# A banded attention, a gated MLP and a mixer on one core: weight conversions at other places, a reciprocal one group earlier

## The chip, the cores and the metric

The kernel runs on one core of one Trainium2 chip. The metric is the device time of one execution in microseconds, as a median of several. The core has five engines that run on their own and meet through semaphores: TensorE (PE, matrix products), VectorE (DVE), ScalarE (ACT), GpSimd (POOL) and SyncE (SP), which here only issues DMA transfers. Each engine takes its instructions strictly in the order in which the program has them, so an instruction that waits holds all that stand behind it.

## The reference

Three parts run one after another on 2 batches of 768 tokens. First an attention with 8 heads of 64, in which a query sees the last `window` keys and the first `n_sink`; then a gated MLP with a spatial gate; then a token and channel mixer.

```python
scores = np.where(keep, scale * q @ k.T, -1e9)            # keep: sinks, or 0 <= rel < window
a = np.exp(scores - max); a = a / (a.sum(-1) + 1e-09)
x = (a @ v) over the heads side by side                   # (2, 768, 512)
h = np.maximum(x @ w_in, 0.0);  u, v = h[..., :512], h[..., 512:]
v_n = (v - mean) / np.sqrt(var + 1e-06)
v_s = np.einsum('ts,bsd->btd', w_spatial, v_n) + b_spatial[None, :, None]
x = (u * v_s) @ w_out
u = x + (np.maximum(x.T @ w_tok1, 0.0) @ w_tok2).T        # token mixing
out = u + np.maximum(u @ w_ch1, 0.0) @ w_ch2              # channel mixing
```

The weights come as 64-bit floats; each 128 x 512 piece is turned into a 32-bit float and then split into a high and a low part, and each product is made of three matmuls (high by high, high by low, low by high).

## The kernel before

**The attention loop** (`banded`) runs over n from -3 to 25. Group n is half of the 8 heads of one block of 128 queries: j = n // 2 is the block (12 of them, 6 for each batch), ph = n % 2 the half. It is a hand-written software pipeline. One pass of the loop issues, in this order: the loads for later blocks (odd n); the reciprocal of the sums of group n+1 (`sums`, L198, VectorE); the transposes of group n (L272, TensorE) and their copies out (L280 on ScalarE, L283 on VectorE); the scaling of two heads of group n+1 on GpSimd (`norm`, L250); the second half of the last weight conversion (`flush`, L506 on ScalarE and L507 on GpSimd); the scaling of the two other heads on ScalarE (L255); the score products of group n+3 (L191) and their masking and minimum on VectorE (L215, L220); the exponentials of group n+2 on ScalarE with their sums (L236, L240); the products with v of group n-1 (L306); and, in even passes, the output of block j-1: `x_out` with L334 on ScalarE and L335 on VectorE. The accumulator `pv` of the products with v has one PSUM buffer, so that the products of the next block wait for L335.

**A weight conversion** (`pump`) takes three operations on VectorE (L488, L492, L495); its `flush` comes one conversion or one pass later: a rounding copy on ScalarE (L506) and a subtraction on GpSimd (L507). Before its work `pump` issues the next load (`prefetch`) on SP's queue, two loads ahead at most. In the loop `pump` is called at the end of the passes in `PUMPS`, eight times: four pieces of `w_in` for v, then four for u.

**The fills.** While attention runs, TensorE also gets the products of the gated MLP, in steps: a v tile (`v_tile`, 128 tokens, four steps of three matmuls of 512 columns, then relu L539, statistics L549 and normalisation L554) and a u tile (`u_tile`, 384 tokens, four steps of 384 columns). A list `self.fills` fixes their order; each pass takes steps from its head up to `BUDGET`, and only if the block that the head needs is done (`xdone`). What is left over runs after the loop.

**After the loop** come the spatial gate, the product with `w_out` (`x2_tile`), the token mixing (`tok1_tile`, `tok2_tile`, with the addition L633 on VectorE) and the channel mixing, three chunks of twelve tiles f: `ch1_tile` (L653 on ScalarE, L654 on VectorE make the two parts of the activated tile) and `ch2_part` of the tile before. The other 38 conversions are called in these stages, each at a fixed place.

Of the kernel before, what the change touches and what calls it, by code (L numbers as in the profile page):

```python
# [29 lines left out]
NG = B * NB * 2  # L30

LQ, LE, LN = 3, 2, 1
PUMPS = range(-1, 7)
BUDGET = 1900


def f32(ap):
    return ap.bitcast(F32)


class Kernel:
# [302 lines left out]
    def banded(self):  # L344
        self.q, self.vb, self.vsb, self.ps_s, self.ss, self.e, self.sm, self.rs = {}, {}, {}, {}, {}, {}, {}, {}
        self.aT, self.ps_x, self.aS, self.dv, self.eS = {}, {}, {}, {}, {}
        NJ = B * NB
        self.kr = self.ap.tile([P, NC4, RING, KW], F32, name="kr")
        self.vf = self.ap, "vf", 2
        self.scalar_loads(self.cp)  # L350
        self.load_qk(0, 2)
        self.warm(10)
        self.load_qk(1)
        self.prefetch()
        self.load_v(0)
        self.load_qk(2)
        self.masks(self.ap)
        for n in range(-LQ, NG + 2):
            j, ph = divmod(n, 2)
            self.xdone = self.xnext  # L360
            if ph and n >= -1:
                if (n + 7) // 2 < NJ:
                    self.load_qk((n + 7) // 2)
                if (n + 3) // 2 < NJ:
                    self.load_v((n + 3) // 2)
            if 0 <= n + LN < NG:
                self.sums(n + LN)
            if 0 <= n < NG:
                self.a_transpose(n)
                self.a_out(n)  # L370
            if 0 <= n + LN < NG:
                self.norm(n + LN, "P")
            if n - 1 in PUMPS:
                self.flush()
            if 0 <= n + LN < NG:
                self.norm(n + LN, "A")
            if n + LQ < NG:
                self.qk(n + LQ)
                if n < 0:
                    self.warm(3)  # L380
                self.scores(n + LQ)
            if 0 <= n + LE < NG:
                self.expo(n + LE)
            if 0 <= n - 1 < NG:
                self.pv(n - 1)
                if ph == 0:
                    if (j - 1) % NB:
                        self.sinks_mm(j - 1)

                    self.fill_until(j - 1)  # L390
                    self.x_out(j - 1)
            if 0 <= n < NG and ph == 0 and j % NB:
                self.v_step(j)
                self.sink_parts(j)
            if n in (2, 3, 14, 15):
                self.split_vs(n // 12, n % 2)
            self.step()
            if n in PUMPS:
                self.pump()
            if 0 <= n < NG and ph == 1 and j % NB:  # L400
                self.sinks(j)
            if n == NG - 4:
                self.raws = [self.spatial_load(r) for r in range(2)]
            self.fill(BUDGET)
        self.xdone = self.xnext
        self.vf = self.sp, "tmp", 4


    def start_x(self):

        self.xT = self.pair(("XH", "XL"), [P, NC4, S], "xT")
        self.w_v = self.pair(("WA", "WB"), [P, NC4, 512], "wv")
        self.w_u = self.pair(("UC", "UD"), [P, NC4, 512], "wu")
        self.wq, self.wstarted, self.wdone, self.half = [], 0, 0, None
        for c in range(NC4):
            self.queue_weight(self.w_in, slice(c * P, c * P + P), (512, 1024), tuple(x[:, c] for x in self.w_v))
        for c in range(NC4):
            self.queue_weight(self.w_in, slice(c * P, c * P + P), (0, 512), tuple(x[:, c] for x in self.w_u))
        self.vn = [self.pair((f"{x}H", f"{x}L"), [P, NB, 512], "vn") for x in "VN"]
        self.uT = [self.unit(f"U{b}", [P, NC4, S], F32, "uT") for b in range(B)]  # L420
        self.xdone = self.xnext = -1
        self.raws = []
        self.later = []

        self.fills = []
        for b in range(B):
            for half in range(2):
                for t in range(3 * half, 3 * half + 3):
                    self.fills.append((b * NB + t, b * NB + t, self.v_tile(b, t)))
                for d in range(NC4):  # L430
                    self.fills.append((b * NB + 3 * half + 2, b * NB + 3 * half, self.u_tile(b, d, half)))
# [41 lines left out]
    def pump(self, n=1):  # L473
        for _ in range(n):
            self.prefetch()
            if self.wdone >= len(self.wq):
                self.flush()
                return
            src, rows, (c0, c1), (dh, dl), raw = self.wq[self.wdone]
            n_ = c1 - c0  # L480
            V = self.nc.vector
            if src.dtype == F32:
                w = raw[:, :n_]
            else:
                r3 = raw.rearrange("p (c w) -> p c w", w=2)
                lo, hi = r3[:, :n_, 0], r3[:, :n_, 1]
                wi = self.sp.tile([P, 512], I32, name="wi", tag="tmp", bufs=4)[:, :n_]
                V.tensor_scalar(  # L488
                    out=wi, in0=hi, scalar1=3, scalar2=0x3FFFFFFF,
                    op0=ALU.logical_shift_left, op1=ALU.bitwise_and,  # L490
                )
                V.scalar_tensor_tensor(  # L492
                    out=wi, in0=hi, scalar=-0x40000000, in1=wi, op0=ALU.bitwise_and, op1=ALU.bitwise_or
                )
                V.scalar_tensor_tensor(  # L495
                    out=wi, in0=lo, scalar=29, in1=wi, op0=ALU.logical_shift_right, op1=ALU.bitwise_or
                )
                w = f32(wi)
            self.flush()
            self.half = w, dh, dl  # L500
            self.wdone += 1
# [168 lines left out]
    def mlp(self):  # L670
        pump = self.pump
# [77 lines left out]
        for n, (b, t) in enumerate(BT):  # L749
            self.tok2_tile(b, t)  # L750
            if 6 <= n <= 9:
                self.u_transpose(n - 6)
            if n == 0:
                self.flush()
            if n >= 9:
                pump()

        self.u2T += [self.pair(("XH", "XL"), [P, NC4, 512], "u2")]
# [2 lines left out]
        for n in range(NCH * NF + 1):  # L761
            if n < NCH * NF:
                ch, f = divmod(n, NF)
                if ch == 1 and f == 0:
                    self.u2T += [self.pair(("NH", "NL"), [P, NC4, 512], "u2")]
                self.ch1_tile(ch, f)
                if ch == 0:
                    pump()
                if 3 <= f < 7 and ch + 1 < NCH:
                    self.u_transpose(4 * (ch + 1) + f - 3)  # L770
            if n >= 1:
                self.ch2_part(*divmod(n - 1, NF))
# [163 lines left out]
```

## Time and profile before

| what | value |
|---|---|
| median of 3 runs | 488.09 us (488.01 to 489.81) |
| the profiled execution | 488.14 us, of which the span from first to last instruction is 486.4 us |
| TensorE busy | 465.6 us, 96% of the span |
| VectorE, ScalarE, GpSimd busy | 273.9, 183.2, 143.5 us |
| load of a piece of `w_in`, issue to landing (median) | 4.5 us |
| load of a piece of `w_ch1` or `w_ch2`, issue to landing (median) | 3.5 us |

How to read it: the span stands 1.7 us below the execution's own time, which is what lies around the first and the last instruction. Busy shares are means over stages with different limits: the attention loop takes the first 135 us, and there the shares are quite different from those of channel mixing, which begins at about 278 us. Matmuls are pipelined, so their listed lengths overlap; the starts of neighbours tell how fast they follow each other.

### The profile page before, as it was taken

What the parts mean: (1) busy time and instruction counts of PE and PEld (TensorE: products, weight loads), DVE (VectorE), ACT (ScalarE), POOL (GpSimd) and SP (SyncE); (2) the same over time, 40 slices, a digit from 0 to 9 for tenths busy, and PEclk for the clock granted to TensorE, in tenths of its full rate; (3) what the DMA queues carried; (4) which work ended last, traced back from release to release, by engine and by line L of the source; (5) the groups of instructions that cost most, each with busy time, mean ns of one, the idle gap of its engine ahead of it and who ended that gap; (6) DMA issues with size and microseconds to landing.
All of it is one profiled execution on the core that took longest, in us unless ns stands there. A gap on an engine that the chain in (4) does not pass through costs nothing.

```text
span 486.4 us, 6920 instructions
## 1 busy us (share of the span) xinstructions
PE 465.6 (96%) x2562; PEld 387.9 (80%) x2562; DVE 273.9 (56%) x609; ACT 183.2 (38%) x507; POOL 143.5 (30%) x164
## 2 busy tenths in 40 slices
PE   8788999999999999999999989999999999999994
PEld 7455677788898999988888768888888888888883
DVE  6988844875446399847988796766312211311112
ACT  4877786796644222235432222211111100010000
POOL 1545641462445466724443042222100000000000
PEclk9899999999999999999999999999999999999998
DMA  8854212212032032205533054221100000200002
GB/s 258 292 174 159 89 64 66 67 29 83 1 117 101 0 109 87 88 0 160 165 130 131 6 169 129 88 86 43 71 17 1 0 1 0 86 1 0 1 0 93
DMA packets 19721, 38.47 MB, mean 79 GB/s; under 512 B 1824, under 2 KB 8224, under 8 KB 19680
## 3 DMA queue, kind: packets, MB, share of 16 engines
q1 hardware_dynamic: 19248, 37.69, 23.5%
q8 instruction: 22, 0.36, 0.3%
q10 hardware_dynamic: 432, 0.26, 0.2%
q14 instruction: 19, 0.16, 0.1%
HBM read 34.80 MB, written 3.15 MB: 78 GB/s over the span
## 4 chain that ended last, share of the span: by engine, by line
PE 81%; DVE 10%; ACT 6%; issue 1%; DMA 1%; POOL 0%; POOLq 0%; ACTq 0%
PE pso L60 7%; PE pso L58 7%; PE pso L59 7%; PE psc L60 6%; PE psc L58 6%; PE psc L59 6%; PE psg L60 3%; PE psg L59 3%; PE psg L58 3%; PE pv L306 3%; PE sc L191 2%; ACT e L236 2%; PE ps L60 2%; PE ps L58 2%; PE ps L59 2%; DVE wi L492 2%
## 5 line engine op out<-in xcount | busy, mean ns | idle before, releaser
L654 DVE SCALAR_TENSOR_TENSOR hh<-psc,hh 128x512 fp32r<-128x512 f32 x36 | 24.9, 691 | 124.8 <-ACT hh L653 124.8
L653 ACT ACTIVATE hh<-psc 128x512 fp32r<-128x512 f32 x36 | 21.5, 597 | 156.2 <-PE psc L60 156.2
L60 PE MATMUL pso<-c2H,hh 128*128 128x512 f32 x144 | 56.3, 391 | 1.9 <-DVE hh L654 1.9
L58 PE MATMUL pso<-c2H,hh 128*128 128x512 f32 x144 | 56.8, 394 | 0.0
L59 PE MATMUL pso<-c2L,hh 128*128 128x512 f32 x144 | 56.1, 389 | 0.0
L495 DVE SCALAR_TENSOR_TENSOR wi<-rawi,wi 128x512 int32<-128x512 int32 (+2 forms) x46 | 39.2, 853 | 1.6
L236 ACT ACTIVATE e<-s,nm 128x136 f32<-128x136 f32 (+1 forms) x96 | 37.6, 394 | 4.0 <-DVE nm L220 4.0
L492 DVE SCALAR_TENSOR_TENSOR wi<-rawi,wi 128x512 int32<-128x512 int32 (+2 forms) x46 | 37.4, 813 | 1.6
L60 PEld LDWEIGHTS pso<-c2H,hh 128*128 128x128 f32 x144 | 27.0, 188 | 8.0 <-DVE hh L654 2.3
L488 DVE TENSOR_SCALAR wi<-rawi 128x512 int32<-128x512 int32 (+2 forms) x46 | 31.4, 682 | 1.6 <-DMA rawi<-in_moe_w_ch 0.9
L58 PE MATMUL psg<-wsTH,vnH 128*128 128x384 f32 x96 | 32.1, 334 | 0.0
L59 PE MATMUL psg<-wsTL,vnH 128*128 128x384 f32 x96 | 32.1, 334 | 0.0
L60 PE MATMUL psg<-wsTH,vnL 128*128 128x384 f32 x96 | 32.1, 334 | 0.0
L59 PEld LDWEIGHTS pso<-c2L,hh 128*128 128x128 f32 x144 | 27.1, 188 | 5.5
L507 POOL TENSOR_TENSOR c2L<-wi,c2H 128x512 fp32r<-128x512 f32 x12 | 15.9, 1321 | 52.7 <-ACT c2H L506 52.7
L58 PEld LDWEIGHTS pso<-c2H,hh 128*128 128x128 f32 x144 | 27.0, 188 | 5.3
L191 PE MATMUL sc<-kr,q 64*128 64x264 f32 (+2 forms) x192 | 28.4, 408 | 0.9 <-DVE nm L220 0.6
L60 PE MATMUL psc<-u2H,c 128*128 128x512 f32 x72 | 28.0, 389 | 0.0
L58 PE MATMUL psc<-u2H,c1H 128*128 128x512 f32 x72 | 28.0, 389 | 0.0
L59 PE MATMUL psc<-u2L,c1H 128*128 128x512 f32 x72 | 28.0, 389 | 0.0
L60 PE MATMUL psc<-u2H,c1L 128*128 128x512 f32 x72 | 28.0, 389 | 0.0
L58 PE MATMUL psc<-u2H,c 128*128 128x512 f32 x72 | 28.0, 389 | 0.0
(143 smaller groups left out, 1107.9 us busy)
## 6 DMA issues: line engine op xcount, KB each, us to landing
rawi<-in_moe_w_ch SPq DMA_DIRECT2D x24, 512.0 KB, 3.5
rawi<-in_moe_w_in SPq DMA_DIRECT2D x8, 512.0 KB, 4.5
v<-in_v SPq DMA_DIRECT2D x12, 256.0 KB, 3.3
out_x<-o SPq DMA_DIRECT2D x12, 256.0 KB, 2.2
kr<-in_k SPq DMA_DIRECT2D x11, 272.0 KB, 4.6
q<-in_q SPq DMA_DIRECT2D x11, 256.0 KB, 4.6
raws<-in_w_spT SPq DMA_DIRECT2D x6, 384.0 KB, 4.0
rawi<-in_moe_w_out SPq DMA_DIRECT2D x4, 512.0 KB, 5.2
```

The lines of the kernel that those rows point to most:

```text
L58: self.nc.tensor.matmul(ps, lh, rh, start=(first and i == 0), stop=False)
L59: self.nc.tensor.matmul(ps, lh, rl, start=False, stop=False)
L60: self.nc.tensor.matmul(ps, ll, rh, start=False, stop=(last and i == n - 1))
L191: nc.tensor.matmul(o, q[r, p, :], k, start=True, stop=True)
L236: nc.scalar.activation(out=self.e[j][:, 4 * ph + c, :u], in_=s[:, c, :u], func=AF.Exp, bias=nm[:, c : c + 1], scale=-1.0, accum_out=sm[:, ...
L306: nc.tensor.matmul(ps[h * D : (h + 1) * D, p, :], w[:, (2 * p + h) * D : (2 * p + h + 1) * D], self.aT[g][c][:, 2 * x + h, :], start=(p == ...
L488: V.tensor_scalar(out=wi, in0=hi, scalar1=3, scalar2=0x3FFFFFFF, op0=ALU.logical_shift_left, op1=ALU.bitwise_and,)
L492: V.scalar_tensor_tensor(out=wi, in0=hi, scalar=-0x40000000, in1=wi, op0=ALU.bitwise_and, op1=ALU.bitwise_or)
L495: V.scalar_tensor_tensor(out=wi, in0=lo, scalar=29, in1=wi, op0=ALU.logical_shift_right, op1=ALU.bitwise_or)
L507: self.nc.gpsimd.tensor_tensor(out=dl, in0=w, in1=f32(dh), op=ALU.subtract)
L653: nc.scalar.activation(out=h, in_=ps, func=AF.Relu)
L654: nc.vector.scalar_tensor_tensor(out=l, in0=ps, scalar=0.0, in1=f32(h), op0=ALU.max, op1=ALU.subtract)
```

## The change

Four things are changed. `PUMPS` keeps the conversions of passes -1 to 3 and takes 5, 7 and 9 in place of 4, 5 and 6. The reciprocal is issued right behind the exponentials of the same group, which on VectorE means behind the scores of the pass, one pass earlier than before. In the first batch the first half of the fills takes four v tiles (0 to 3) and then the u tiles, and the second half v tiles 4 and 5. The last conversion of token mixing goes, and tile f = 1 of the first chunk of channel mixing gets two.

```diff
-PUMPS = range(-1, 7)
+PUMPS = (-1, 0, 1, 2, 3, 5, 7, 9)
...
-            if 0 <= n + LN < NG:
-                self.sums(n + LN)
             if 0 <= n < NG:
                 self.a_transpose(n)
...
                 self.expo(n + LE)
+                self.sums(n + LE)
...
-                for t in range(3 * half, 3 * half + 3):
+                for t in range(3 * half + (b == 0 and half), 3 * half + 3 + (b == 0 and not half)):
...
-            if n >= 9:
+            if 9 <= n < 11:
                 pump()
...
-                    pump()
+                    pump(2 if f == 1 else 1)
```

Three places show what moves on VectorE. The first is the end of pass -1 (passes 0 and 1 alike); `r` is the tile of reciprocals, `sums` that of the sums, `wi` the piece that is being converted, `nm` the negative maximum.

```order
 L220 ISA nm 128x1
-L488 TENSOR_SCALAR wi<-rawi 128x512
-L492 SCALAR_TENSOR_TENSOR wi<-rawi,wi 128x512
-L495 SCALAR_TENSOR_TENSOR wi<-rawi,wi 128x512
-L198 RECIPROCAL r<-sums 128x4
+L198 RECIPROCAL r<-sums 128x4
+L488 TENSOR_SCALAR wi<-rawi 128x512
+L492 SCALAR_TENSOR_TENSOR wi<-rawi,wi 128x512
+L495 SCALAR_TENSOR_TENSOR wi<-rawi,wi 128x512
 L215 COPY_PREDICATED sc<-low,sc 128x2x128
```

The reciprocal has moved from behind the conversion to ahead of it; it is the same group's.

The second is the end of pass 4, on VectorE: `xTL` is the low part of the output of block 1, `st` the statistics of v tile 0.

```order
 L220 ISA nm 128x1
+L198 RECIPROCAL r<-sums 128x4
 L335 TENSOR_TENSOR xTL<-pv,xTH 128x4x128
-L488 TENSOR_SCALAR wi<-rawi 128x512
-L492 SCALAR_TENSOR_TENSOR wi<-rawi,wi 128x512
-L495 SCALAR_TENSOR_TENSOR wi<-rawi,wi 128x512
-L549 BN_STATS st<-vf 128x6
-L550 BN_AGGR st<-st 128x2
-L198 RECIPROCAL r<-sums 128x4
+L549 BN_STATS st<-vf 128x6
+L550 BN_AGGR st<-st 128x2
 L283 TENSOR_TENSOR aL<-tr,lowT 128x512
```

The conversion between L335 and the statistics is gone, and the reciprocal stands ahead of L335.

The third is VectorE where token mixing ends and channel mixing begins, before:

```order
L633 TENSOR_TENSOR x2f<-pst,x2f 128x512
L488 TENSOR_SCALAR wi<-rawi 128x512
L492 SCALAR_TENSOR_TENSOR wi<-rawi,wi 128x512
L495 SCALAR_TENSOR_TENSOR wi<-rawi,wi 128x512
L654 SCALAR_TENSOR_TENSOR hh<-psc,hh 128x512
```

and in the changed kernel:

```order
L633 TENSOR_TENSOR x2f<-pst,x2f 128x512
L654 SCALAR_TENSOR_TENSOR hh<-psc,hh 128x512
L488 TENSOR_SCALAR wi<-rawi 128x512
L492 SCALAR_TENSOR_TENSOR wi<-rawi,wi 128x512
L495 SCALAR_TENSOR_TENSOR wi<-rawi,wi 128x512
```

The first tile of channel mixing (`hh`) now follows the last addition of token mixing directly. On ScalarE and GpSimd the copy and the subtraction of each moved conversion follow it. On TensorE the nine matmuls of u tile 0 that closed pass 8 are gone from there: four steps of v tile 3 come in passes 9 and 10, and u tile 0 behind them.

## Rows read from the trace of the kernel before

In a row of a timeline: start in us from the span's first instruction, length in us, engine, line, operation, tile written <- tiles read, shapes; in brackets the engine's idle time ahead of it and what ended that.

**Rows 1.** busy time by stretch (us; x instructions), then granted clock, DMA share, GB/s

```profile
core 0: us, PE busy (x) PEld busy (x) DVE busy (x) ACT busy (x) POOL busy (x), PEclk, DMA share, GB/s
11.00:66.00 55.00, 45.24 (x339) 31.43 (x339) 45.85 (x162) 42.34 (x154) 30.20 (x40) 0.97 0.51 166
66.00:264.00 198.00, 197.49 (x1208) 173.24 (x1206) 136.97 (x297) 100.79 (x277) 91.64 (x99) 1.00 0.25 83
277.00:288.00 11.00, 9.10 (x40) 7.24 (x39) 10.72 (x15) 2.87 (x5) 4.09 (x3) 1.00 0.46 139
```

**Rows 2.** timeline, VectorE, groups 0 and 1: start, length, operation, [idle before]

```profile
13.74 0.17 DVE L198 RECIPROCAL r<-sums 128x4 f32<-128x4 f32 x1
...
15.61 0.51 DVE L488 TENSOR_SCALAR wi<-rawi 128x512 int32<-128x512 int32 x1
...
17.49 0.17 DVE L198 RECIPROCAL r<-sums 128x4 f32<-128x4 f32 x1
```

**Rows 3.** timeline, ScalarE, groups 0 to 5

```profile
13.85 0.63 ACT L506 ACTIVATE wvH<-wi 128x512 fp32r<-128x512 f32 x1 [1.34 <-DVE wi L495]
...
16.67 0.21 ACT L240 ACTIVATE sums<-sums 128x4 f32<-128x4 f32 x1
...
21.39 0.63 ACT L506 ACTIVATE wvH<-wi 128x512 fp32r<-128x512 f32 x1 [0.27 <-DVE wi L495]
...
30.29 0.20 ACT L240 ACTIVATE sums<-sums 128x4 f32<-128x4 f32 x1
...
38.62 0.63 ACT L506 ACTIVATE wuH<-wi 128x512 fp32r<-128x512 f32 x1 [1.43 <-DVE wi L495]
...
41.81 0.20 ACT L240 ACTIVATE sums<-sums 128x4 f32<-128x4 f32 x1
```

**Rows 4.** timeline, VectorE, groups 2 to 8

```profile
24.94 0.69 DVE L335 TENSOR_TENSOR xTL<-pv,xTH 128x512 fp32r<-128x512 f32 x1 [1.12 <-ACT xTH L334]
...
29.92 0.68 DVE L161 TENSOR_TENSOR vs<-vsraw,vs 32x512 fp32r<-32x512 f32 x1
...
41.76 0.72 DVE L554 TENSOR_SCALAR vf<-vf,st 128x512 f32<-128x512 f32 x1
...
48.92 1.65 DVE L492 SCALAR_TENSOR_TENSOR wi<-rawi,wi 128x512 int32<-128x512 int32 x1
...
51.21 0.69 DVE L549 BATCH_NORM_STATS2 st<-vf 128x6 f32<-128x512 f32 x1
...
55.15 0.16 DVE L198 RECIPROCAL r<-sums 128x4 f32<-128x4 f32 x1
...
58.40 0.69 DVE L335 TENSOR_TENSOR xTL<-pv,xTH 128x512 fp32r<-128x512 f32 x1 [0.40 <-ACT xTH L334]
```

**Rows 5.** timeline, GpSimd, groups 1 and 6

```profile
17.74 0.64 POOL L250 TENSOR_TENSOR e<-e,r 128x272 f32<-128x272 f32 x1 [1.90 <-DVE r L198]
...
48.57 1.45 POOL L558 TENSOR_TENSOR vnL<-vf,vnH 128x512 fp32r<-128x512 f32 x1
```

**Rows 6.** timeline, TensorE, groups 8 to 10

```profile
57.62 0.34 PE L58 MATMUL psu<-xTH,wuH 128*128 128x384 f32 x1
...
59.20 0.60 PE L272 MATMUL tr<-ident,e 128*128 128x128 f32 x4
...
65.06 0.60 PE L272 MATMUL tr<-ident,e 128*128 128x128 f32 x4
```

**Rows 7.** chain that ended last: start, length, what

```profile
66.31 1.02 PE pv L306 x16
...
92.86 0.35 PE fl L316 x2
```

**Rows 8.** timeline, VectorE then TensorE, where channel mixing begins

```profile
282.36 0.42 DVE L488 TENSOR_SCALAR wi<-rawi 128x512 int32<-128x512 int32 x1
...
285.13 0.68 DVE L654 SCALAR_TENSOR_TENSOR hh<-psc,hh 128x512 fp32r<-128x512 f32 x1
...
285.87 0.50 PE L60 MATMUL pso<-c2H,hh 128*128 128x512 f32 x1 [1.90 <-DVE hh L654]
```

## The prediction

> **What bounds the kernel now.** I read the busy time by stretch first. TensorE sets the time nearly everywhere: from 66 to 264 us it is busy for 197.49 of 198.00, but in the attention loop from 11 to 66 us only for 45.24 of 55.00, and where channel mixing begins, 277 to 288 us, for 9.10 of 11.00 [rows 1]. The work of TensorE is the same before and after (the same matmuls, in another order), so the end can move only by these two gaps: some 9.8 us in the loop, 1.9 us at the second place. The timelines then say who makes the gaps. In the loop no engine is full, but VectorE and ScalarE release each other in a ring. A weight conversion on VectorE ends, and ScalarE, idle until then, starts its rounding copy L506, with 1.34 and 1.43 of idle time ahead of it [rows 3]. Behind that copy on ScalarE stand the scaling L255, four exponentials and the sum L240, and in even groups the output copy L334, for which VectorE's L335 waits (1.12 idle) [rows 4]. Only then does VectorE go on, to the next conversion. "Group n" below is the pass n of the loop, "conversion(n)" the one issued in it; conversion(n) is rounded on ScalarE in pass n+1.
>
> **Part 1: the reciprocal earlier.** Today reciprocal(n+1) opens pass n. Its sum is long done, so it costs only its own 0.1 us or so: VectorE runs from 13.74 to 17.49, 3.75 a pass, without a hole [rows 2]. Afterwards VectorE takes reciprocal(n+2) right behind the scores of pass n, and ahead of conversion(n). Its sum is L240 of the same pass on ScalarE, and this stands behind the rounding copy of conversion(n-1). That closes a shorter ring: conversion ends, copy starts at 13.85, L240 runs from 16.67 to 16.88 [rows 3], then the reciprocal, then conversion(0), which today starts at 15.61 [rows 2]. So conversion(0) is 16.88 - 15.61 = 1.3 late. A turn of the ring is 16.88 - 13.74 = 3.1 from the end of one conversion to the sum, plus 0.1 for the reciprocal, plus the conversion, 17.49 - 15.61 = 1.9, together 5.1 against 3.75 today: pass 1 loses another 1.3. In pass 2 L335 waits for the same ScalarE row anyway, so nothing is added. In pass 3 L240 ends at 30.49 [rows 3], where VectorE today goes on with L161 at 29.92 [rows 4]: 0.6. Sum **+3.2**. What is queued behind the waiting reciprocal is the conversion, and who waits for that is ScalarE with the next exponentials. What the earlier reciprocal gives, that L255 and GpSimd's L250 need not wait for it, is worth little: the ring is held by the copy in front of them.
>
> GpSimd's scaling L250 starts 0.25 us after the reciprocal starts and takes 0.64 (17.74 against 17.49) [rows 2, 5]. Today it runs beside the mask and score operations; afterwards beside the conversion. Beside GpSimd's L558 (48.57 to 50.02) the conversion's L492 took 1.65 and ended 0.55 after it [rows 4, 5]; undisturbed it takes 0.69 (conversion(0): 1.88 in all, 0.51 of it L488, the rest for L492 and L495 alike). By the same distance, L492 would end 0.25 + 0.64 + 0.55 = 1.44 after the reciprocal's start, instead of 0.1 + 0.51 + 0.69 = 1.3; with GpSimd itself slowed a little by L488 (L558 beside it 1.45), I take 0.3. For passes -1 to 2 that is **+1.2**; bounds: 0, and four times 1.65 - 0.69, 3.8. I take 1.2 because L250 is half as long as L558. The Trainium skill (GPSIMD Engine Reference, section 8, Key points) says that GpSimd shares its SBUF interfaces with VectorE and contends with instructions in a two-port mode or with two SBUF inputs. By that rule L161 of pass 3 would be slowed too and the forecast 0.3 higher; no row here has GpSimd beside it.
>
> **Part 2: conversions every second pass.** Those of passes 4 and 6 go away, 5 stays, 7 and 9 get one; their copies on ScalarE and subtractions on GpSimd follow one pass later. Conversion(4) stood on VectorE between L335 and the statistics: **-1.9** (the 1.9 above). Conversion(6) held L492 from 48.92 and the statistics started at 51.21, 2.3, with some 0.5 of L488 ahead: 2.8 [rows 2, 4]. Afterwards the statistics meet ScalarE's relu of the v tile, which the conversion hides today, so I take **-2.2** (bounds 1.9 and 2.8). Conversion(7) is new: **+1.9**. By the end of pass 7, where VectorE today stands at 55.15 [rows 4], the shift is 3.2 + 1.2 - 1.9 - 2.2 + 1.9 = +2.2: 57.35. And pass 8 now starts with a rounding copy. From the end of a conversion to L335 it is 3.65: 0.1 to the copy (13.85 - 13.74) and 24.94 - 21.39 [rows 2 to 4], so L335 of block 3 starts at 61.0, today 58.40.
>
> The loads of the moved conversions go behind two or three k, q and v loads on SP's queue. A load of w_in lands 4.5 us after its issue (table of the profile), and the next conversion is now a period of some 10 us away: nothing.
>
> **Part 3: v ahead of u.** After L335 of block 3 (0.65 long) TensorE has its way free: 16 products of 1.02, two transposes of 0.35 [rows 7] and three steps of v. A step of u is 1.58 / 3 = 0.53 (57.62 to 59.20); a v step with 512 instead of 384 columns 0.70 [rows 6]. So the transposes of pass 10 start at 61.65 + 1.02 + 0.35 + 2.1 = 65.1; today 65.06 [rows 6]. TensorE stands there at the same time, but with other work done: today u has had seven steps by then (3.7), afterwards only three of v (2.1), since the fourth v tile is not ready in pass 8 and u stands behind it. Deferred: **+1.6**, paid later, when TensorE is full. Conversion(9) and its copy in pass 10 still hold L335 of the next block; TensorE then has v and u steps in front, so I take **+0.3** (bounds 0 and 1.9). From there TensorE is the bound as today. The loop: 0.0 + 1.6 + 0.3 = **+1.9**.
>
> **Part 4: the moved conversion.** Today conversion L488 to L495 starts at 282.36 between the last x2f and L654, which therefore starts at 285.13; TensorE waits 1.90 for it, until 285.87 [rows 8]. Without it L654 starts at 282.36, ends at 283.0, and TensorE wants it at 285.87 - 1.90 = 283.97: the wait goes, **-1.9**, with 0.9 to spare. The conversion comes back as the second one of the next but one tile, where VectorE, whose turn of a conversion and an L654 is 2.8 + 0.6, is ahead of TensorE by then: 0. Its load lands 3.5 us after its issue (table) and a conversion here takes 285.13 - 282.36 = 2.8, so it may come 0.7 late; the same margin holds that.
>
> **The sum.** +1.9 - 1.9 = 0.0 against the profiled execution's 488.14 us (486.4 of span and 1.7 around it); that execution stands 0.05 over the median of 488.09. Forecast **488.1**: two edits that cancel.
>
> **Rivals.**
> A, the loop gains (faster): ScalarE would have its sum ready before VectorE is through its scores, so neither the +3.2 nor the contention is paid, 488.1 - 4.4 = 483.7. For it: ScalarE idles over 1.3 us ahead of its copy. Against: that idle time ends with the conversion, so it is no reserve; the reciprocal needs what comes after.
> B, the ring closes in passes 5 and 7 too (slower): there no copy stands ahead of the exponentials. Today L240 of pass 5 ends at 42.01 and VectorE's scores are through at 41.76, where L554 starts [rows 3, 4]. Without the copy (1.43 idle, 0.63 of copy [rows 3]) ScalarE comes 2.1 sooner, VectorE without conversion(4) 1.9 sooner: almost a draw. If ScalarE comes out later, each of the two passes loses up to the 1.3 of pass 0: 488.1 + 2.6 = 490.7. It decides as soon as the sum trails the scores by more than the few tenths of today.
> C, the gain of part 4 does not come, because L653 on ScalarE or something else holds L654: 490.0. Against: only the conversion stands between.
>
> **Chances.** Forecast 0.62, A 0.15, B 0.15, C 0.08. A measurement of this kernel tells about 0.5%, 2.4 us, from no change: under 485.7 is faster, over 490.5 slower. A is faster, B slower, C and the forecast neither: 0.15, 0.70, 0.15. The range takes the forecast with its bounds (contention from 0, -1.2, to about twice my value, +1.2; conversion(9) up to +1.6; conversion(6) -0.5) and reaches B: 485.5 to 490.8, leaving out most of A.
>
> **What would show it.** Part 1 holds if VectorE's reciprocals in passes 0, 1 and 3 have idle time ahead of them that ends with L240, and conversion(0) starts near 16.9 or later; it is wrong if they start without a hole. The contention shows as L492 over 0.9 us in passes -1 to 2. Part 2: L335 of block 3 near 61. Part 3: transposes of pass 10 near 65, and TensorE's busy share from 11 to 66 below today's. Part 4: no wait of TensorE for L654. The forecast fails if the loop ends earlier at the same stock of v and u steps.

## The result: 492.2 us, slower, where no change was forecast

The changed kernel takes **492.23 us** (median of 5 runs, 491.95 to 492.63) against 488.09 of the kernel before beside it: a ratio of 1.0067, interval 1.0048 to 1.0085. The forecast was 488.1, with a range from 485.5 to 490.8. Its two parts, an attention loop that loses and a channel mixing that gains, are both there; the forecast made the loss too small. The executions of the kernel before fall into two groups, near 488 and near 490, and the profiled one (488.14) is of the first, so that marks below are compared with that one.

Busy time by stretch of the changed kernel (us; x instructions, then granted clock, DMA share, GB/s):

```profile
11.00:66.00 55.00, 44.53 (x308) 30.98 (x307) 44.78 (x154) 39.38 (x145) 28.01 (x37) 0.86 0.51 164
66.00:126.00 60.00, 58.79 (x456) 47.78 (x455) 37.43 (x152) 45.14 (x168) 25.75 (x36) 0.99 0.19 62
277.00:292.00 15.00, 14.85 (x70) 11.80 (x70) 12.73 (x19) 4.26 (x7) 2.66 (x2) 1.00 0.22 70
```

Against [rows 1], TensorE's hole where channel mixing begins is closed. The attention loop is where the time went, and the first row understates it: the mean granted clock is 0.86 of full speed, and at the lower clock the same products are listed longer (four of L306 with 0.70 at a clock of 0.50, see 63.67 below, and with 0.44 at full clock, at 62.98 in the run with idle products). So I follow marks instead of shares: L335 of each block, the transposes of group 10, the first product of channel mixing (`psc`), and the product that waited for L654 in [rows 8].

VectorE's timeline of the changed kernel, passes 0, 1 and 3, and the conversions of passes 3 and 5:

```profile
17.30 0.18 DVE L198 RECIPROCAL r<-sums 128x4 f32<-128x4 f32 x1 [1.28 <-ACT sums L240]
17.39 0.40 DVE L488 TENSOR_SCALAR wi<-rawi 128x512 int32<-128x512 int32 x1
17.82 1.01 DVE L492 SCALAR_TENSOR_TENSOR wi<-rawi,wi 128x512 int32<-128x512 int32 x1
...
22.72 0.18 DVE L198 RECIPROCAL r<-sums 128x4 f32<-128x4 f32 x1 [1.36 <-ACT sums L240]
...
34.53 0.18 DVE L198 RECIPROCAL r<-sums 128x4 f32<-128x4 f32 x1 [0.77 <-ACT sums L240]
34.74 0.68 DVE L161 TENSOR_TENSOR vs<-vsraw,vs 32x512 fp32r<-32x512 f32 x1
35.45 0.75 DVE L488 TENSOR_SCALAR wi<-rawi 128x512 int32<-128x512 int32 x1
36.24 0.69 DVE L492 SCALAR_TENSOR_TENSOR wi<-rawi,wi 128x512 int32<-128x512 int32 x1
...
45.08 0.17 DVE L198 RECIPROCAL r<-sums 128x4 f32<-128x4 f32 x1
45.16 0.52 DVE L554 TENSOR_SCALAR vf<-vf,st 128x512 f32<-128x512 f32 x1
45.60 0.87 DVE L488 TENSOR_SCALAR wi<-rawi 128x512 int32<-128x512 int32 x1
```

and GpSimd's scaling in passes 0, 3 and 5 of it:

```profile
17.55 0.73 POOL L250 TENSOR_TENSOR e<-e,r 128x272 f32<-128x272 f32 x1 [1.32 <-DVE r L198]
...
34.78 1.14 POOL L250 TENSOR_TENSOR e<-e,r 128x272 f32<-128x272 f32 x1 [1.38 <-DVE r L198]
...
45.33 0.85 POOL L250 TENSOR_TENSOR e<-e,r 128x272 f32<-128x272 f32 x1 [0.98 <-DVE r L198]
```

The ring is there: the reciprocal waits for the sum, by 1.28 and 1.36 in the passes for which 1.3 each was forecast, and a turn is 22.72 - 17.30 = 5.42 instead of the 3.75 of [rows 2]. GpSimd's L250 now runs beside the conversion: L492 takes 1.01 where it starts before L250 ends. From pass 3 on it is L488 that is hit, 0.75 to 0.87 against 0.42 undisturbed: that collision the forecast did not have.

The marks, VectorE then TensorE of the changed kernel:

```profile
28.56 0.69 DVE L335 TENSOR_TENSOR xTL<-pv,xTH 128x512 fp32r<-128x512 f32 x1 [0.24 <-ACT xTH L334]
41.24 0.69 DVE L335 TENSOR_TENSOR xTL<-pv,xTH 128x512 fp32r<-128x512 f32 x1 [0.24 <-ACT xTH L334]
52.15 0.69 DVE L335 TENSOR_TENSOR xTL<-pv,xTH 128x512 fp32r<-128x512 f32 x1 [0.31 <-ACT xTH L334]
62.93 0.69 DVE L335 TENSOR_TENSOR xTL<-pv,xTH 128x512 fp32r<-128x512 f32 x1 [0.31 <-ACT xTH L334]
```

```profile
63.67 0.70 PE L306 MATMUL pv<-aT,v 128*64 128x128 f32 x4 [1.29 <-DVE xTL L335]
...
68.63 0.60 PE L272 MATMUL tr<-ident,e 128*128 128x128 f32 x4
...
284.60 0.39 PE L58 MATMUL psc<-u2H,c1H 128*128 128x512 f32 x1
...
290.49 0.39 PE L60 MATMUL pso<-c2H,hh 128*128 128x512 f32 x1
```

In the kernel before, VectorE then TensorE:

```profile
36.10 0.69 DVE L335 TENSOR_TENSOR xTL<-pv,xTH 128x512 fp32r<-128x512 f32 x1 [1.12 <-ACT xTH L334]
47.86 0.69 DVE L335 TENSOR_TENSOR xTL<-pv,xTH 128x512 fp32r<-128x512 f32 x1 [1.12 <-ACT xTH L334]
```

```profile
277.92 0.39 PE L58 MATMUL psc<-u2H,c1H 128*128 128x512 f32 x1
```

The last mark has no wait any more. It is 290.49 - 285.87 = 4.62 late and `psc` 6.68, so the attention costs 6.7 and channel mixing gives 2.1 back. The span grew by the same, 490.9 - 486.4 = 4.5.

### The profile page after: what moved, and what is told of

It is laid out like the page before. It is cut to its first block, busy times and chain, and to the rows that moved or that the text cites. A ratio compares the mean times of both kernels' runs of the same rounds, so it can differ in the third digit from the quotient of the medians.

```text
span 490.9 us, 6924 instructions
## 1 busy us (share of the span) xinstructions
PE 470.9 (96%) x2562; PEld 393.1 (80%) x2562; DVE 274.8 (56%) x609; ACT 183.1 (37%) x507; POOL 145.9 (30%) x164
## 4 chain that ended last, share of the span: by engine, by line
PE 80%; ACT 10%; DVE 6%; issue 1%; DMA 1%; POOL 0%; DVEq 0%; POOLq 0%; ACTq 0%
PE pso L60 7%; PE pso L58 7%; PE psc L60 7%; PE pso L59 7%; PE psc L59 7%; PE psc L58 7%; ACT e L236 4%; PE psg L60 3%; PE psg L59 3%; PE psg L58 3%; PE pv L306 3%; PE ps L60 2%; PE ps L58 2%; PE ps L59 2%; PE psu L58 2%; PE psu L60 2%
## 5 line engine op out<-in xcount | busy, mean ns | idle before, releaser
L654 DVE SCALAR_TENSOR_TENSOR hh<-psc,hh 128x512 fp32r<-128x512 f32 x36 | 24.9, 691 | 122.6 <-ACT hh L653 122.6
L492 DVE SCALAR_TENSOR_TENSOR wi<-rawi,wi 128x512 int32<-128x512 int32 (+2 forms) x46 | 39.8, 865 | 1.6
L495 DVE SCALAR_TENSOR_TENSOR wi<-rawi,wi 128x512 int32<-128x512 int32 (+2 forms) x46 | 38.2, 830 | 1.6
L488 DVE TENSOR_SCALAR wi<-rawi 128x512 int32<-128x512 int32 (+2 forms) x46 | 31.2, 679 | 2.5 <-DMA rawi<-in_moe_w_ch 2.4
L507 POOL TENSOR_TENSOR c2L<-wi,c2H 128x512 fp32r<-128x512 f32 x12 | 15.8, 1314 | 50.4 <-ACT c2H L506 50.4
L191 PE MATMUL sc<-kr,q 64*128 64x264 f32 (+2 forms) x192 | 29.6, 427 | 0.3 <-DVE nm L220 0.3
L60 PE MATMUL psc<-u2H,c 128*128 128x512 f32 x72 | 28.1, 390 | 0.0
L59 PE MATMUL psc<-u2L,c 128*128 128x512 f32 x72 | 28.0, 389 | 0.0
```

The source lines that it names most:

```text
L59: self.nc.tensor.matmul(ps, lh, rl, start=False, stop=False)
L60: self.nc.tensor.matmul(ps, ll, rh, start=False, stop=(last and i == n - 1))
L191: nc.tensor.matmul(o, q[r, p, :], k, start=True, stop=True)
L488: V.tensor_scalar(out=wi, in0=hi, scalar1=3, scalar2=0x3FFFFFFF, op0=ALU.logical_shift_left, op1=ALU.bitwise_and,)
L492: V.scalar_tensor_tensor(out=wi, in0=hi, scalar=-0x40000000, in1=wi, op0=ALU.bitwise_and, op1=ALU.bitwise_or)
L495: V.scalar_tensor_tensor(out=wi, in0=lo, scalar=29, in1=wi, op0=ALU.logical_shift_right, op1=ALU.bitwise_or)
```

## Experiments

The theory: the reciprocal's ring and the collision that comes with it make the whole loss. Rivals: TensorE's lower clock makes it; the new order of the fills; the later passes. Each run has 5 rounds beside the kernel before, in three batches: the median of before was 489.21 beside the reciprocal alone, everything but it, channel mixing alone and the idle products; 489.22 beside the order of the fills, the second reciprocal and the first two late copies; and 488.78 beside the other four. The changed kernel itself ran in a batch of its own (488.09 beside it), so what sets a run against it rests on the ratios and on the marks.

### The reciprocal alone

Kernel before, and of the change only this:

```diff
-            if 0 <= n + LN < NG:
-                self.sums(n + LN)
...
                 self.expo(n + LE)
+                self.sums(n + LE)
```

> The kernel before with the reciprocal alone moved; conversions, fills and channel mixing as before. Ring theory (the reciprocal behind the scores of the same pass closes a ring conversion, rounding copy, exponentials, sum, reciprocal, conversion): every pass with a conversion ahead of it loses 1 to 1.6 us, some 5 us by pass 3 as in the changed kernel, more in pass 5; 493 to 496 us, and TensorE's granted clock falls in the longer gaps. Rival (the conversions' new places and the order v before u cause the loss): 487 to 489 us.

Measured 494.37, ratio 1.0106 (1.0082 to 1.0130): slower than the whole change, with intervals that just overlap. From 11 to 80 us VectorE's reciprocals wait 7.4 us for the sums. `psc` stands at 283.19, so in the loop this run loses 5.3, less than the 6.7 of the changed kernel. The rest lies behind `psc`: TensorE's wait for L654 is still there (1.89), and behind it, in the profiled execution (495.17), the granted clock is at 0.50 from 293 to 295 us, 0.89 over 284 to 300. From `psc` to the end it takes 493.3 - 283.19 = 210.1 us, against 486.4 - 277.92 = 208.5 in the profiled execution of the kernel before, which has the same wait and keeps a clock of 1.00 from 284 to 300.

### Everything but the reciprocal

The changed kernel, with that edit undone.

> The changed kernel with the reciprocal where it was before; the other three edits stay. Ring theory: the loss goes and what is left is a gain, 483.5 to 485.5 us. Rival (conversions and v before u): still slower than before, 489 to 492 us, with the granted clock falling between 40 and 47 us as in the changed kernel.

Measured 485.61, ratio 0.9936 (0.9914 to 0.9958): 6.6 us below the changed kernel, and 0.1 above the range given. The marks in it:

```profile
56.24 0.69 DVE L335 TENSOR_TENSOR xTL<-pv,xTH 128x512 fp32r<-128x512 f32 x1 [1.12 <-ACT xTH L334]
```

```profile
60.34 0.60 PE L272 MATMUL tr<-ident,e 128*128 128x128 f32 x4
...
70.54 0.44 PE L58 MATMUL psu<-xTH,wuH 128*128 128x384 f32 x1 [1.58 <-ACT aS L318]
...
277.38 0.39 PE L58 MATMUL psc<-u2H,c1H 128*128 128x512 f32 x1
```

So the move costs 284.60 - 277.38 = 7.2 us here. The rest of the change brings the transposes of group 10 4.7 us earlier than before, and `psc` only 0.5.

### Channel mixing alone

```diff
-            if n >= 9:
+            if 9 <= n < 11:
                 pump()
...
-                    pump()
+                    pump(2 if f == 1 else 1)
```

> The kernel before with only the conversion moved from token mixing into channel mixing. All theories: TensorE's wait of 1.9 us for L654 goes and nothing comes in its place, 486.1 us; if VectorE's double conversion in tile 1 holds a later tile, 487 to 488.

Measured 485.92, ratio 0.9938 (0.9916 to 0.9960): this one edit does as well as everything but the reciprocal. `psc` stands at 277.87, as before, and TensorE's wait for L654 is gone.

### v ahead of u alone

```diff
-                for t in range(3 * half, 3 * half + 3):
+                for t in range(3 * half + (b == 0 and half), 3 * half + 3 + (b == 0 and not half)):
```

> The kernel before with only the order of the fills changed (four v tiles, then u, in the first batch). If the order is the loss beside the ring: three u steps fewer by pass 10 (1.6 us) and u tiles that wait for a PSUM buffer behind L318, 490 to 491 us. If it costs nothing because pass 8 gets shorter by the same steps: 487.5 to 488.5 us.

Measured 490.67, ratio 1.0020 (1.0005 to 1.0035); `psc` at 278.59, 0.7 late, in a profiled execution of 488.90. The order alone gives nothing and costs a little. The new places of the conversions were not run alone; they are part of everything but the reciprocal, which is faster.

### Is it the clock?

In the changed kernel TensorE drops to the lower of its two levels behind its waits; the windows show it at 0.50 (1.2 of 2.4 GHz) around 43 and 65 us. From 36.0 to 40.5 us, ahead of the first, it is busy for 2.81 of 4.50, and ahead of the second stands the wait of 1.29 at 63.67.

```profile
40.50:46.00 5.50, 5.00 (x26) 3.56 (x25) 4.84 (x18) 4.42 (x17) 2.98 (x7) 0.50 0.05 21
48.00:63.00 15.00, 14.12 (x118) 10.34 (x117) 11.75 (x44) 12.42 (x46) 9.11 (x11) 1.00 0.48 152
63.70:66.50 2.80, 2.80 (x20) 2.36 (x21) 2.29 (x11) 2.80 (x12) 2.54 (x4) 0.50 0.02 5
```

The experiment fills its gaps with 30 products of the identity that nobody reads:

```diff
+            if n in (1, 2, 3, 5):
+                self.warm({1: 8, 2: 5, 3: 8, 5: 5}[n])
             if 0 <= n < NG:
                 self.a_transpose(n)
...
+                if n == 9:
+                    self.warm(4)
                 self.pv(n - 1)
```

> The changed kernel with idle matmuls of the identity (nobody reads them) put into TensorE's gaps ahead of the transposes of passes 1, 2, 3, 5 and of the products of pass 9, 30 in all. If the fallen clock costs time by itself, the granted clock stays at 1.00 from 30 to 66 us and some 2 us come back: 489.8 to 490.5 us. If the ring alone sets the loss and the clock costs nothing: 492 to 493 us.

Measured 492.40, ratio 1.0065 (1.0043 to 1.0086): not faster, at a clock restored over the whole loop:

```profile
11.00:66.00 55.00, 47.81 (x375) 35.00 (x374) 45.03 (x155) 40.14 (x148) 28.55 (x37) 1.00 0.52 165
```

```profile
66.35 0.60 PE L272 MATMUL tr<-ident,e 128*128 128x128 f32 x4
...
77.05 0.44 PE L58 MATMUL psu<-xTH,wuH 128*128 128x384 f32 x1 [1.55 <-ACT aS L318]
```

The transposes of group 10 come 2.3 earlier (66.35 against 68.63), but TensorE then waits 1.55 instead of 0.50 for ScalarE's copy `aS`, and `psc` comes out at 283.87, 0.7 earlier. The clock's loss is mostly taken where TensorE would have waited anyway.

### The collision taken away, the ring kept

The changed kernel; GpSimd's scaling gets a second reciprocal, issued on VectorE at the old place:

```diff
         if on == "P":
+            r = self.rp[g]
...
+            if 0 <= n + LN < NG:
+                self.rp[n + LN] = self.ap.tile([P, 4], F32, name="rp", tag="rp", bufs=3)
+                self.nc.vector.reciprocal(self.rp[n + LN], self.sm[n + LN])
             if 0 <= n < NG:
                 self.a_transpose(n)
```

> The changed kernel, but GpSimd's scaling L250 takes a second reciprocal that is issued where it stood before, so that it no longer runs beside the conversion; ScalarE's scaling keeps the moved one and the ring stays closed. If the collision of L250 with L488 and L492 (0.3 to 0.45 us in each of eight conversions in the trace of the changed kernel) reaches the end: 489.5 to 490.5 us, and L492 back at 0.69, L488 at 0.42. If it is hidden: 491.5 to 492.5 us.

Measured 489.44, ratio 1.0006 (0.9993 to 1.0020). The conversion is undisturbed again, from VectorE's timeline:

```profile
17.42 0.40 DVE L493 TENSOR_SCALAR wi<-rawi 128x512 int32<-128x512 int32 x1
17.85 0.69 DVE L497 SCALAR_TENSOR_TENSOR wi<-rawi,wi 128x512 int32<-128x512 int32 x1
...
34.41 0.43 DVE L493 TENSOR_SCALAR wi<-rawi 128x512 int32<-128x512 int32 x1
```

VectorE's waits for the sum, from 11 to 80 us, stay at 8.1, and the first product of channel mixing comes earlier:

```profile
281.20 0.39 PE L58 MATMUL psc<-u2H,c1H 128*128 128x512 f32 x1
```

So of the 7.2, 284.60 - 281.20 = 3.4 go with the collision and 281.20 - 277.38 = 3.8 are left for the ring. The split holds for this order, the collision taken away first.

### The ring opened, the collision kept

The changed kernel, with the rounding copy and the subtraction moved behind the exponentials and the output copy:

```diff
-            if n - 1 in PUMPS:
-                self.flush()
...
+            if n - 1 in PUMPS:
+                self.flush()
             if 0 <= n < NG and ph == 0 and j % NB:
                 self.v_step(j)
```

> The changed kernel with the rounding copy L506 and the subtraction L507 issued behind the exponentials and the output copy of the same pass instead of ahead of them. If the ring closes through that copy, as the theory says, the reciprocals of passes 0, 1 and 3 start without waiting and the time falls to 483.5 to 486 us. If ScalarE's exponentials alone make the reciprocal late: 490 us or more.

Measured 486.39, ratio 0.9945 (0.9928 to 0.9963), `psc` at 277.96; the time is 0.4 above the range given. From 11 to 80 us VectorE's waits for the sum shrink from 8.2 to 1.1. This shows that the sum was late because it stood behind the copy. And the collision goes on (pass 0 of it on VectorE):

```profile
16.34 0.99 DVE L488 TENSOR_SCALAR wi<-rawi 128x512 int32<-128x512 int32 x1
17.37 1.01 DVE L492 SCALAR_TENSOR_TENSOR wi<-rawi,wi 128x512 int32<-128x512 int32 x1
```

yet `psc` is only 277.96 - 277.38 = 0.6 behind the run without the reciprocal's move, whatever the late copy itself costs or gives included. So the two parts do not add up independently: the 3.4 are the collision's price while the ring is closed, when everything waits for the end of the conversion.

### The same late copy elsewhere: three misses

First on the kernel before with the channel-mixing edit:

> The kernel before with the conversion moved into channel mixing and the rounding copy behind the exponentials and the output copy; reciprocal, conversions and fills as before. If the copy ahead of the exponentials is also what holds L335 in the kernel before: L335 of block 1 starts a microsecond or more before 36.1, 483 to 485 us. If VectorE alone bounds the loop: 485.5 to 486.5 us, as without it.

Measured 493.40, ratio 1.0081 (1.0065 to 1.0097), a miss: worse by far. GpSimd's subtraction L507 moves with the copy, and beside the next conversion it does what L250 did, at twice the length; and TensorE waits 6.3 us for `dv`, the cause of the next miss. VectorE, then GpSimd, pass 4 of it:

```profile
38.63 1.51 DVE L488 TENSOR_SCALAR wi<-rawi 128x512 int32<-128x512 int32 x1
40.17 1.63 DVE L492 SCALAR_TENSOR_TENSOR wi<-rawi,wi 128x512 int32<-128x512 int32 x1
```

```profile
38.59 1.27 POOL L507 TENSOR_TENSOR wuL<-wi,wuH 128x512 fp32r<-128x512 f32 x1 [2.91 <-ACT wuH L506]
39.81 1.44 POOL L290 TENSOR_TENSOR dv<-v 128x512 f32<-128x512 f32 x1
```

Then on everything but the reciprocal, in passes 4 and later alone, where no conversion follows directly:

> The changed kernel with the reciprocal in its old place, and in passes 4 and later the rounding copy and subtraction of a conversion behind the exponentials and the output copy. Theory (TensorE is full from pass 9 on and L335 comes sooner before that): 484.5 to 485.6. Rival (the late subtraction on GpSimd runs beside the next work of VectorE and slows it, as it did where every pass has a conversion): 486 to 489.

Measured 492.14, ratio 1.0060 (1.0037 to 1.0082), outside both guesses. The conversions keep their 0.41 and 0.69; what is late is `dv`, which stands behind the subtraction on GpSimd and which TensorE's products with v need. GpSimd and TensorE, pass 4:

```profile
36.17 1.28 POOL L510 TENSOR_TENSOR wuL<-wi,wuH 128x512 fp32r<-128x512 f32 x1 [2.91 <-ACT wuH L509]
37.41 1.27 POOL L290 TENSOR_TENSOR dv<-v 128x512 f32<-128x512 f32 x1
```

```profile
38.73 0.44 PE L306 MATMUL pv<-aL,dv 128*64 128x128 f32 x4 [1.94 <-POOL dv L290]
```

Last with both cures at once, the second reciprocal and the late copy:

> The changed kernel with both halves of the loss taken away: GpSimd's scaling takes a second reciprocal, issued at the old place, so that it does not run beside the conversion; and the rounding copy stands behind the exponentials and the output copy, so that the sum does not wait for it. Theory (contention and ring together are the whole loss of the reciprocal's move): 484.5 to 486.5, that is the changed kernel without the move (485.6) or slightly above for the extra reciprocals. Rival (the move costs something else, such as the wait for the exponentials themselves): 487.5 or more.

Measured 487.64, ratio 0.9958 (0.9942 to 0.9974). It lies just inside the rival's side, though the causes named there are small: waits for the sum are 1.8 us from 11 to 80 us, and TensorE waits 5.1 for `dv` (2.6 with the late copy alone). The late copy has its own price, so this run can't settle the sum of the two parts; the split above rests on the second reciprocal and on the run without the move.

### Early or late passes, and one conversion later

The changed kernel with the reciprocal in its old place up to pass 3 and in the new one from pass 4:

```diff
+            if 0 <= n + LN < NG and n < 5:
+                self.sums(n + LN)
...
                 self.expo(n + LE)
-                self.sums(n + LE)
+                if n >= 4:
+                    self.sums(n + LE)
```

> The changed kernel with the reciprocal in its old place for the groups of passes -1 to 3, and one group ahead only from pass 4 on. Theory (the ring of conversion, rounding copy, sum and reciprocal costs most in passes -1 to 3, where every pass has a conversion): 486.0 to 488.0 us. Rival (the later passes 5, 7 and 9 carry as much): 488.5 to 490.5. If only the early passes count: 485.0 to 486.0, as without the reciprocal.

Measured 487.23, ratio 0.9963 (0.9950 to 0.9977), `psc` at 278.85. So 284.60 - 278.85 = 5.7 of the 7.2 come from passes -1 to 3, and 278.85 - 277.38 = 1.5 from the later ones.

And the kernel before with the channel-mixing edit and the last conversion in pass 7 instead of 6:

```diff
-PUMPS = range(-1, 7)
+PUMPS = (-1, 0, 1, 2, 3, 4, 5, 7)
```

> The kernel before with the conversion moved into channel mixing and the last conversion of the loop from pass 6 to pass 7; reciprocal and fills as before. Theory (TensorE is the bound from pass 6 on, so that a place of one conversion gives little): 485.4 to 486.2, as with the channel-mixing edit alone (485.9). Rival (conversion(6) collides with the GpSimd subtraction of v tile normalisation, L558, and at pass 7 it does not): 484.5 to 485.4.

Measured 487.21, ratio 0.9958 (0.9942 to 0.9975), `psc` at 279.51, 1.6 later than without the shift, in a profiled execution of 487.47 (the fastest of nine took 485.98): better by neither theory. A new u tile now waits 2.27 for its buffer:

```profile
63.45 0.69 PE L58 MATMUL psu<-xTH,wuH 128*128 128x384 f32 x1 [2.27 <-ACT aS L318]
```

Of the versions that beat both kernels, the fastest are channel mixing alone (485.92) and everything but the reciprocal (485.61); they can't be told apart.

## Why the prediction was wrong, step by step

| step | predicted | changed kernel | without the reciprocal's move |
|---|---|---|---|
| L335 of block 0 (pass 2), against before | +3.5 | +3.6 | 0.0 |
| L335 of block 1 (pass 4) | +4.4 | +5.1 | 0.0 |
| L335 of block 2 (pass 6) | +2.5 | +4.3 | -2.0 |
| L335 of block 3 (pass 8) | +2.6 | +4.5 | -2.2 |
| transposes of group 10 | 0.0 | +3.6 | -4.7 |
| `psc`, the loop's end in it | +1.9 | +6.7 | -0.5 |
| channel mixing (last mark less `psc`) | -1.9 | -2.1 | -2.1 |

The predicted column is the prediction's own terms, added up to each mark.

**Part 1, the ring: right, a little small.** Passes -1 to 1 came as forecast, wait by wait. Over the loop the ring measures 3.8 against +3.2. It does not close in pass 5 or 7 (45.08 above has no wait ahead of it), so rival B's mechanism is not the cause, though its time was the nearest.

**Part 1, the collision: the term that failed first.** "For passes -1 to 2 that is +1.2" holds for these passes: L492 takes 0.98 to 1.01, 0.3 more each. But the step left out that the reciprocal also stands just ahead of the conversions of passes 3, 5, 7 and 9, where L250 meets L488: +0.3 in pass 3, +0.4 each in the others, and the whole is 3.4 instead of 1.2 (in the order of the experiments above). The upper bound of 3.8 would have held it; the value chosen did not count the passes. The kernel before already showed L488 being hit: the 0.51 that the prediction takes for it is 0.42 elsewhere, and that L488 ends 0.28 after GpSimd's L507 (16.12 against 15.84). The Trainium skill (GPSIMD Engine Reference, section 8, Key points) names the contention of GpSimd with VectorE's two-port and two-input instructions. The forecast took this as L161 of pass 3 slowed; it took its 0.68, and GpSimd's L250 beside it took 1.14 instead of 0.64. So the trace agrees that the two can't both run at speed, but here GpSimd, which started 0.04 later (34.78 against 34.74), was the one that was held.

**Part 2: right.** Without the reciprocal's move, L335 of blocks 2 and 3 is 2.0 and 2.2 early; the prediction's terms are -1.9 and -1.8. With it, another 1.1 is lost in passes 5 and 6, to the collision of L488 and to an L283 that waits 0.83 for the copy of transposes which TensorE made late at the lower clock (with the clock restored that wait is gone, and L335 of block 2 starts at 51.46, 0.7 earlier).

**Part 3: the place was right, "from there TensorE is the bound as today" failed.** Without the reciprocal's move, the transposes of group 10 start at 60.34; the prediction without part 1 gives 65.1 - 4.4 = 60.7. Then 4.7 shrinks to 0.5. Of these 4.2, 1.6 are the deferred u steps, as forecast. Another 2.0 are waits after 66 us: a new u or v tile takes the PSUM buffer that the sink transposes (L316) hold until ScalarE's copy L318, which stands behind four exponentials. The windows show it, before and then without the reciprocal's move:

```profile
66.00:126.00 60.00, 59.68 (x472) 48.23 (x469) 37.56 (x148) 47.18 (x176) 22.87 (x37) 1.00 0.19 62
```

```profile
66.00:126.00 60.00, 57.70 (x450) 46.56 (x452) 34.81 (x140) 44.71 (x164) 22.56 (x38) 1.00 0.16 50
```

TensorE's idle time is 0.32 and 2.30, and rows like that of 70.54 above (1.58, then twice 0.36) are all of it. I read TensorE as full there because it was full in the kernel before; a TensorE that comes earlier meets a ScalarE that does not. The only term for waits there was +0.3, for conversion(9), with a bound of 1.9. The remaining 0.6 of the 4.2 is no wait: from the transposes of group 10 to `psc` TensorE is busy for 214.46 us without the move and for 212.24 before, 2.2 more where the deferred steps were put at 1.6; which products make the difference I can't assign.

**The sum.** The loop was forecast at +1.9 and is +6.7. Of the 4.8 that are missing, 7.2 - 4.4 = 2.8 are part 1 (2.2 the collision, 0.6 the ring) and 2.0 are what parts 2 and 3 did not bring, -0.5 instead of -2.5. The forecast was too low in both places. The run without the move shows the second by itself. The first depends on the rest of the change: with the reciprocal alone `psc` is 283.19 - 277.92 = 5.3 late, not far from the 4.4 of the forecast, and only beside the other edits it is 7.2; what makes the 1.9 between them was not taken apart.

**Part 4: right.** TensorE's wait of 1.90 is gone and 2.1 came back; rival C fell. Alone, that edit makes the median 0.62% shorter.

**Rival A fell** with the first two waits of the reciprocals: ScalarE's idle time (1.84 and 1.91 ahead of L506 in passes 1 and 2) ended with the conversion, as the prediction said against it.

**The lower clock** was not in the prediction. It explains the 1.6 between L335 of block 3 and the transposes of group 10 (5.7 instead of the 4.1 at full clock in the run without the move), but at most 0.7 of it reached `psc`, below what the medians can tell.

## What to carry to other kernels

Before moving an instruction earlier in an in-order queue, ask what its operand stands behind on the other engine: a cheap reciprocal that waits for a sum behind a copy of the last conversion makes a ring out of two engines that only brushed each other. Count a collision in every place where the new order puts the pair side by side, and price it by whether the slowed engine is in the ring at that time. And where a part of the change lets the full engine come earlier, look for the buffers and copies that were on time only because it was late.

## What the runs showed of the hardware

**VectorE's conversion ends at a fixed distance behind GpSimd's operation.** In the changed kernel L492 ends 0.55 after L250 in every early pass (18.83 against 18.28, and at the same distance in passes 1 and 2), L488 0.28 to 0.29 after it in later ones (36.20 against 35.92, 46.47 against 46.18); with the late copy on the kernel before, L488 ends 0.28 after L507 (40.14 against 39.86) and L492 0.55 after L290 (41.80 against 41.25). Undisturbed they take 0.69 and 0.42. So the price was not a share of the overlap but set by GpSimd's end, as if the operation on VectorE had stood until GpSimd was nearly through. In all of these GpSimd's operation had started first. Where VectorE's had (L161 at 34.74, L250 at 34.78), it kept its length, and GpSimd's ended 0.50 behind it (35.92 against 35.42).

**A lower clock can cost nothing, or all of it.** TensorE ran at the lower level for some 15 us of the loop in the changed kernel (0.86 of full speed over 55 us), and bringing the clock back moved its work by 2.3 us at one mark, 0.7 at the end, and nothing in the median. TensorE was waiting for others in between, and the time saved became waiting time. With the reciprocal alone the clock fell in channel mixing, where TensorE waits for nothing afterwards, and there the stretch from `psc` to the end became 1.6 us longer.
